# Batch 1's keys and values by plain transfers and halvings on GpSimd; batch 2's keys accumulated between the halvings

## The chip, the cores and the metric

The kernel runs on one core of a Trainium2 chip. The metric is the device time of one execution in microseconds (us); the time of a kernel is the median of its runs. The profile is of one execution, taken by the hardware profiler. Engines are called as the profile calls them: PE is TensorE's matmuls, PEld its weight loads, DVE is VectorE, ACT is ScalarE, POOL is GpSimd, SP is SyncE; the DMA queue that SP issues to is SPq.

## What is computed

Attention with pooled keys and values (8 batches, 8 heads, 576 tokens, 64 channels; groups of 8 keys and of 8 values are averaged, which leaves 72 of each), followed by a feed-forward layer with a squared ReLU, from 512 to 2048 and back to 512:

```python
Sp = S // pool                                    # 576 // 8 = 72
k_p = k.reshape(B, H, Sp, pool, D).mean(axis=3)
v_p = v.reshape(B, H, Sp, pool, D).mean(axis=3)
scores = scale * np.matmul(q, k_p.transpose(0, 1, 3, 2))
attn = np.exp(scores - np.max(scores, axis=-1, keepdims=True))
attn = attn / (np.sum(attn, axis=-1, keepdims=True) + 1e-09)
attn_out = np.matmul(attn, v_p).astype(np.float32)
x = np.ascontiguousarray(attn_out.transpose(0, 2, 1, 3)).reshape(B * S, H * D)
h = np.maximum(x @ w_in, 0.0)
out = (h * h @ w_out).astype(np.float32)
```

The two weight matrices come as 64-bit floats, so the kernel reads 16.8 MB of weights and makes float32 of them itself.

## The kernel before, in words

**Tiling.** The 4608 tokens are cut into 9 chunks of 512 (`c`). A chunk's feed-forward layer goes in 16 steps (`fc`), each for 128 of the 2048 hidden channels: `h_c_fc` is the product with `w_in`, `r` is ACT's ReLU and square of it, and `o` is the product with `w_out`, three steps later (`LAG`). A step `s` is `c * 16 + fc`. Step `s` issues on PE first `h` of step `s`, then the attention work that is due at `s`, then `o` of step `s - 3`. Chunk 0 lies wholly in batch 0; chunk 1 needs the last 64 tokens of batch 0 and 448 tokens of batch 1; chunk 2 needs batches 1 and 2.

**Weights.** The raw pieces, 512 KB each, are called `raw_i` (of `w_in`) and `raw_o` (of `w_out`), 32 in all. `land` loads one, `magnitude` has two ACT instructions on it, and `to_float32` three DVE instructions (one TENSOR_SCALAR and two SCALAR_TENSOR_TENSOR with two inputs each), which give `wf_i` or `wf_o`. Eight pieces are loaded ahead of all steps (`EAGER`); the others are due at steps that are worked out backwards from when PE needs them, two per step, loaded two or three steps ahead of their conversion.

**Order.** Every engine executes its instructions in the order in which they are written. In a step, the list `work` holds what is due; on DVE and ACT the attention's parts come first, then pooling, conversions and weights, and the ReLU of the step (`activate`) stands behind the step's `magnitude` calls. The SP queue too is in order: an issue that waits holds all behind it, and an issue waits until the transfer eight places ahead of it has landed (eight semaphores in turn).

**Keys and values.** Batch 0's come as whole rows (`load_pair`: tiles `k8`, `v8`, one for each pair of heads, 288 KB), and chunk 0's queries as four transfers `qn` of 256 KB between the first of them. DVE reduces three pairs of keys (`reduce_k`); POOL does the rest by halvings (`by_halves`: three additions a pair, over 512, 256 and 128 columns). From batch 1 on, the keys and values come as sums made by the DMA: `load_sums` loads one pair of rows of each group in a plain transfer (144 KB) and adds the other three with accumulating transfers, which POOL issues (`GP.dma_start`, tiles `k2`, `v2`, two halves `n` of four heads each), and `pool` adds the last two columns' halves on DVE. An accumulating transfer is issued only when the one before it on its half has landed. The pooled keys are `kq`, the pooled values `vp`. `turn_k` transposes the keys on PE (`kps`): at step 3 for batch 1, at step 8 for batch 2. Values of batch 1 are used on PE (`weigh_values`, `av`) from step 7 on, and the softmax weights `te` of chunk 1 are normalised on DVE at step 5 and transposed on PE (`pps`) at step 6. Scores of chunk 1 are `sps`.

**What is around the change.** The loads ahead of the steps stand in lines 686 to 702, the prologue's POOL work in lines 728 to 737, batch 1's accumulations of values and its two poolings in lines 789 to 794, and batch 2's and later batches' in `kv_steps` (lines 817 to 824). Most large tiles come from one pool of 40 buffers (`w_tile`, `SLOTS`), so that a later load can wait for the last reader of a buffer.

Of the kernel before, what the change touches and what calls it, by code (L numbers as in the profile page):

```python
# [9 lines left out]
F32 = mybir.dt.float32  # L10
# [27 lines left out]
def pooled_attn_relu2_ffn(  # L38
# [22 lines left out]
    POOL = 8  # L61
    SP_ = S // POOL
    NPAIR = H // 2
# [9 lines left out]
    PLAIN = 2  # L73
# [10 lines left out]
    EARLY = ((-13, -12, -8, -7), (0, 1, 2, 3, 4))  # L84
    HALF_AT = ((0, 1, 3, 6, 8), (1, 2, 5, 7, 9))
    KV_AT = (("k", -35), ("v", -27))
    NEXT_AT = {"k": ((3, 4, 5, 6, 7), (3, 4, 5, 6, 7)), "v": ((7, 8, 9, 11, 13), (7, 8, 10, 12, 14))}
    X_AT = (("B11", -9), ("B22", -2), ("T1", -2), ("T3", -2), ("T2", -1), ("B21", -1), ("T4", -1))
    STIR, AWAKE = 10, (2, 2, 0)

# [12 lines left out]
    def load(dst, src):  # L103
        loads.append((dst, src))
# [11 lines left out]
    def w_tile(dt, name):  # L116
        return wts.tile([P, 2, 512], dt, name=name, tag="w", bufs=SLOTS)
# [13 lines left out]
    def land(key):  # L131
        t = raw[key] = w_tile(U32, "raw_" + "_".join(map(str, key)))
        if key[0] == "i":
            _, g, kh, r = key
            n = GB * P
            load(t, w_in[kh * 2 * P:(kh + 1) * 2 * P, (2 * g + r) * n:(2 * g + r + 1) * n].rearrange("(c p) n -> p c n", p=P))
        else:
            load(t.rearrange("p a n -> p (a n)"), w_out[key[1] * P:(key[1] + 1) * P, :])
# [89 lines left out]
    def load_pair(kind, b, p):  # L228
        t = loaded[kind, b, p] = w_tile(F32, f"{kind}8_{b}_{p}")[:SP_]
        load(t, {"k": k, "v": v}[kind][b, 2 * p:2 * p + 2].rearrange("h (s o) d -> s h (o d)", o=POOL))  # L230
# [9 lines left out]
    def halve_k(b, p):  # L240
        if p == 0:
            loaded["kq", b] = sb.tile([SP_, H, D], F32, name=f"kq_{b}", tag="kq", bufs=1)
        kp = loaded["kp", b, p] = loaded["kq", b][:, 2 * p:2 * p + 2, :]
        by_halves(kp, loaded.pop(("k", b, p)))

    def halve_v(b, p):
        new_batch(b)
        by_halves(kv[b][:, 2 * p:2 * p + 2, :], loaded.pop(("v", b, p)))
# [7 lines left out]
    two, started, HALF = {}, set(), H // 2  # L256

    def load_sums(kind, b, n, j):

        if (kind, b) not in started:  # L260
            started.add((kind, b))
            if kind == "k":
                loaded["kq", b] = sb.tile([SP_, H, D], F32, name=f"kq_{b}", tag="kq", bufs=1)
        src = {"k": k, "v": v}[kind][b].rearrange("h (s j o) d -> j s h (o d)", j=POOL // 2, o=2)[j][:, n * HALF:(n + 1) * HALF]
        if b < PLAIN:
            if j == 0 and n == 0:
                t = w_tile(F32, f"{kind}2_{b}")
                for i in range(2):
                    two[kind, b, i] = t[:SP_, i, :].rearrange("s (h x) -> s h x", h=HALF)
            dst = two[kind, b, n]  # L270
        elif j == 0:
            dst = two[kind, b, n] = sb.tile([SP_, HALF, 2 * D], F32, name=f"{kind}2_{b}_{n}", tag="two", bufs=2)
        else:
            dst = two[kind, b, n]
        if j == 0:
            load(dst, src)
        else:
            GP.dma_start(dst, src, accum_op=ALU.add)
# [394 lines left out]
    steps = [(c, fc) for c in range(NCH) for fc in range(NFC)]  # L673
    work = {}

    def at(step, f, *a):
        work.setdefault(max(step, -PRO), []).append((f, a))
# [15 lines left out]
    load_pair("v", 0, 2)  # L693
    load_pair("v", 0, 3)
    land(keys[1])
    for n in range(2):
        load_sums("k", 1, n, 0)
    for key in keys[2:EAGER]:
        land(key)
    for n in range(2):  # L700
        load_sums("v", 1, n, 0)
    issue_loads()


# [23 lines left out]
    for p in range(3):  # L728
        reduce_k(0, p)
    halve_k(0, 3)  # L730
    more = [(n, j) for j in range(1, POOL // 2) for n in range(2)]
    for p in range(NPAIR):
        halve_v(0, p)
        if p == 1:
            load_sums("k", 1, *more.pop(0))
    for n, j in more:
        load_sums("k", 1, n, j)

    st = [None] * NPAIR
    st[0] = turn_rows(0, 0)  # L740
# [45 lines left out]
    to_float32(*keys[2:FIRST])  # L786
    begin(3)

    v_sums = [(n, j) for j in range(1, POOL // 2) for n in range(2)]
    for i, (n, j) in enumerate(v_sums):  # L790
        at(i // 2, load_sums, "v", 1, n, j)
    for n in range(2):
        at(2, pool, "k", 1, n)
        at(5, pool, "v", 1, n)
    at(3, turn_k, 1)
    at(6, split_k, 1)

# [1 line left out]
    t = 1e9  # L799
    for key in reversed(keys):  # L800
        t = min(t - 1 / RATE, need[key] - 1 - MARGIN)
# [15 lines left out]
    def kv_steps(b, s):  # L817
        for kind, start in KV_AT:
            for n in range(2):
                steps = NEXT_AT[kind][n] if b == PLAIN else [s + start + d for d in HALF_AT[n]]  # L820
                for j in range(POOL // 2):
                    at(steps[j], load_sums if j else first_sums, kind, b, n, j)
                at(steps[-1], pool, kind, b, n)
        at(8 if b == PLAIN else s + KV_AT[1][1] + 3, turn_k, b)
# [4 lines left out]
    for c in range(1, NCH):  # L829
# [10 lines left out]
        for p in range(NPAIR):  # L840
            s = c * NFC + first[p]
# [8 lines left out]
    for s in range(-PRO, len(steps) + LAG):  # L850
# [8 lines left out]
        if store:  # L859
            store()  # L860
            send_outs()
        store = project(*steps[s - LAG]) if s >= LAG else None
        if s % 2:
            catch_up()
        if soon:
# [66 lines left out]
```

## Time and profile before

| | us |
|---|---|
| median of 3 runs | 965.21 |
| lowest, highest | 958.71, 965.79 |
| time of the profiled execution | 962.24 |
| its span, first to last instruction | 960.5 |
| PE busy | 904.6 (94%) |
| DVE busy | 559.5 (58%) |
| ACT busy | 511.9 (53%) |
| POOL busy | 405.1 (42%) |

The mean granted TensorE clock of the profiled execution is 0.974 of full speed. Each timeline row has start, length, engine, line, operation, output and input tiles, shapes and count, and in brackets the idle time of the engine before it with what ended it. As nearly every instruction is issued through one helper, all have line 34: the tile names tell them apart. A row of the stretches has, for each engine, busy time and number of instructions, then the granted clock, the DMA engines' busy share and the rate in GB/s.

### The profile page before, as it was taken

The numbers are of one execution on the slowest core, as the hardware profiler recorded it, in microseconds if no ns is written. First come the engines' busy times: TensorE is split into PE (matmuls) and PEld (weight loads), VectorE is DVE, ScalarE is ACT, GpSimd is POOL, SyncE is SP. The second block draws the span as 40 slices with busy tenths as digits, with TensorE's granted clock in tenths as the row PEclk, the third lists the DMA queues.
The fourth block names the chain that finished last, engine by engine and source line by source line (L and its number), as shares of the span: only waits on it lengthen the run. The fifth ranks groups of instructions, "written<-read, shape, count | busy, mean of one in ns | idle before, by whom it ended". The sixth has DMA issues, their size and how long they took to land.

```text
span 960.5 us, 14101 instructions
## 1 busy us (share of the span) xinstructions
PE 904.6 (94%) x5082; PEld 719.8 (75%) x5082; DVE 559.5 (58%) x944; ACT 511.9 (53%) x1019; POOL 405.1 (42%) x215
## 2 busy tenths in 40 slices
PE   8809779999999899999999999999999999999998
PEld 5304334457777788888888888888888888889996
DVE  7705547745677787856575568556744563343321
ACT  5805436746555656565465546554654564444343
POOL 3412232545555446565665565656444444200000
PEclk8958889999999999999999999999999999999999
DMA  9986336468764655576657665755353443234501
GB/s 227 261 210 135 37 55 179 137 151 227 216 161 110 155 137 142 125 178 161 134 123 192 152 142 136 179 142 129 112 169 96 133 121 133 100 136 174 228 1 45
DMA packets 162088, 138.73 MB, mean 144 GB/s; under 512 B 95785, under 2 KB 128041, under 8 KB 162017
## 3 DMA queue, kind: packets, MB, share of 16 engines
q1 hardware_dynamic: 128416, 125.36, 43.4%
q0 software_dynamic: 33600, 12.46, 11.3%
q8 instruction: 40, 0.66, 0.3%
q14 instruction: 32, 0.25, 0.1%
HBM read 119.65 MB, written 18.06 MB: 143 GB/s over the span
## 4 chain that ended last, share of the span: by engine, by line
PE 69%; issue 9%; DVE 9%; DMA 6%; ACT 3%; POOL 3%; SPq 1%; DVEq 0%; ACTq 0%; POOLq 0%
PE o L34 34%; PE h L34 30%; DMA k<-in_k_dram 3%; PE sps L34 3%; PE av L34 2%; DMA w_o<-kept 2%; DVE wf_i L34 1%; POOL k L34 1%; POOL v L34 1%; DVE gl L34 1%; DVE xf L34 1%; DVE wf_o L34 1%; DVE st L34 1%; DMA rb<-rd 1%; ACT sc L34 1%
## 5 line engine op out<-in xcount | busy, mean ns | idle before, releaser
L34 PE MATMUL o<-w_o,gh 128*128 128x512 f32 x1024 | 322.2, 396 | 1.8 <-DMA w_o<-kept 1.7
L34 POOL PARTITION_ALL_REDUCE tot<-sc x56 | 190.1, 3443 | 85.0 <-issue 82.4
L34 PEld LDWEIGHTS o<-w_o,gh 128*128 128x128 f32 x1024 | 184.3, 188 | 46.8 <-issue 6.1
L34 PE MATMUL o<-w_o,gl 128*128 128x512 f32 x512 | 200.9, 392 | 0.0
L34 PE MATMUL h<-x_T,w_S 128*128 128x256 f32 x1008 | 130.9, 283 | 3.8 <-ACT r L34 3.0
L34 ACT ACTIVATE r<-h 128x512 f32<-128x512 f32 x144 | 83.4, 593 | 94.7 <-PE h L34 75.9
L34 POOL PARTITION_ALL_REDUCE mx<-sc x56 | 109.2, 1994 | 54.5 <-ACT sc L34 52.7
L34 PEld LDWEIGHTS h<-x_T,w_S 128*128 128x128 f32 x1008 | 125.0, 190 | 4.6 <-ACT r L34 3.2
L34 PEld LDWEIGHTS o<-w_o,gl 128*128 128x128 f32 x512 | 96.2, 188 | 21.1 <-DVE gl L34 0.2
L34 POOL DMA_DIRECT2D k<-in_k_dram x42 | 51.4, 1223 | 141.4 <-issue 91.7
L34 POOL DMA_DIRECT2D v<-in_v_dram x42 | 51.7, 1230 | 133.3 <-issue 57.0
L34 DVE TENSOR_TENSOR h<-h,u 128x256 f32<-128x256 f32 x168 | 72.7, 433 | 60.0 <-ACT u L34 31.7
L34 ACT COPY u<-h 128x256 f32<-128x256 f32 x112 | 41.8, 373 | 118.4 <-PE h L34 71.9
L34 PE MATMUL h<-x_B,w_A 128*128 128x256 f32 x672 | 98.6, 283 | 0.2 <-ACT r L34 0.2
L34 DVE TENSOR_TENSOR gl<-r,gh 128x512 fp32r<-128x512 f32 x128 | 94.4, 773 | 6.0 <-ACT gh L34 5.9
L34 PEld LDWEIGHTS h<-x_B,w_A 128*128 128x128 f32 x672 | 91.7, 189 | 5.3 <-ACT r L34 0.6
L34 ACT ACTIVATE r<-r 128x512 f32<-128x512 f32 x144 | 84.3, 625 | 1.1
L34 DVE TENSOR_TENSOR u<-h,u 128x256 f32<-128x256 f32 x56 | 23.4, 417 | 103.5 <-ACT u L34 103.5
L34 DVE TENSOR_TENSOR st<-qs,st 64x512 fp32r<-64x512 f32 x56 | 46.3, 826 | 58.7 <-ACT st L34 57.9
L34 ACT CAST gh<-r 128x512 fp32r<-128x512 f32 x128 | 78.9, 617 | 0.9 <-PE o L34 0.7
L34 ACT ACTIVATE sc<-sc 72x512 f32<-72x512 f32 x56 | 34.5, 632 | 67.2 <-DVE sc L34 67.2
L34 PE MATMUL o<-wf_o,r 128*128 128x512 f32 x128 | 64.3, 650 | 0.0
(93 smaller groups left out, 1183.4 us busy)
## 6 DMA issues: line engine op xcount, KB each, us to landing
w_o<-kept SPq DMA_DIRECT2D x128, 512.0 KB
out_dram<-ob SPq DMA_DIRECT2D x36, 256.0 KB
raw_i<-in_moe_w_in_dram SPq DMA_DIRECT2D x16, 512.0 KB
raw_o<-in_moe_w_out_dram SPq DMA_DIRECT2D x16, 512.0 KB
kept<-w_o SPq DMA_DIRECT2D x16, 512.0 KB
rb<-rd SPq DMA_DIRECT2D x56, 128.0 KB
k<-in_k_dram POOLq DMA_DIRECT2D x42, 144.0 KB, 5.4
v<-in_v_dram POOLq DMA_DIRECT2D x42, 144.0 KB, 5.5
```

Source lines behind the costliest of these rows:

```text
L34: return lambda *a, **k: self.tc.keep_in_program_order(f(*a, **k))
```

## The change

Batch 1's keys and values are loaded as whole rows, like batch 0's, behind the first eight weight pieces; POOL halves all eight pairs in the prologue. Batch 2's two plain key transfers move to the prologue as well, and their six accumulating transfers stand between and behind the halvings of batch 1's values. Of batch 2's keys only `pool` stays in the steps, at step 7 for both halves. In steps 0 and 1 the ReLU comes ahead of the step's `magnitude` calls.

```diff
-    NEXT_AT = {"k": ((3, 4, 5, 6, 7), (3, 4, 5, 6, 7)), "v": ((7, 8, 9, 11, 13), (7, 8, 10, 12, 14))}
+    NEXT_AT = ((7, 8, 9, 11, 13), (7, 8, 10, 12, 14))
...
-        if b < PLAIN:
-            if j == 0 and n == 0:
-                t = w_tile(F32, f"{kind}2_{b}")
-                for i in range(2):
-                    two[kind, b, i] = t[:SP_, i, :].rearrange("s (h x) -> s h x", h=HALF)
-            dst = two[kind, b, n]
-        elif j == 0:
+        if j == 0:
             dst = two[kind, b, n] = sb.tile([SP_, HALF, 2 * D], F32, name=f"{kind}2_{b}_{n}", tag="two", bufs=2)
...
     land(keys[1])
-    for n in range(2):
-        load_sums("k", 1, n, 0)
     for key in keys[2:EAGER]:
         land(key)
+    for p in range(NPAIR):
+        load_pair("k", 1, p)
+    for p in range(NPAIR):
+        load_pair("v", 1, p)
     for n in range(2):
-        load_sums("v", 1, n, 0)
+        load_sums("k", PLAIN, n, 0)
     issue_loads()
...
     halve_k(0, 3)
+    for p in range(NPAIR):
+        halve_v(0, p)
+    for p in range(NPAIR):
+        halve_k(1, p)
     more = [(n, j) for j in range(1, POOL // 2) for n in range(2)]
     for p in range(NPAIR):
-        halve_v(0, p)
-        if p == 1:
-            load_sums("k", 1, *more.pop(0))
+        load_sums("k", PLAIN, *more.pop(0))
+        halve_v(1, p)
     for n, j in more:
-        load_sums("k", 1, n, j)
+        load_sums("k", PLAIN, n, j)
...
-    v_sums = [(n, j) for j in range(1, POOL // 2) for n in range(2)]
-    for i, (n, j) in enumerate(v_sums):
-        at(i // 2, load_sums, "v", 1, n, j)
-    for n in range(2):
-        at(2, pool, "k", 1, n)
-        at(5, pool, "v", 1, n)
...
-                steps = NEXT_AT[kind][n] if b == PLAIN else [s + start + d for d in HALF_AT[n]]
+                if b == PLAIN and kind == "k":
+                    at(NEXT_AT[n][0], pool, kind, b, n)
+                    continue
+                steps = NEXT_AT[n] if b == PLAIN else [s + start + d for d in HALF_AT[n]]
...
         store = project(*steps[s - LAG]) if s >= LAG else None
+        if activate and s < 2:
+            activate()
+            activate = None
```

In the orders below, the numbers behind a name are batch and pair or half, and last the buffer's own number.

SP's queue before, from the second raw piece to the first that is due in the steps (`k2_1` and `v2_1` are the plain first transfers of batch 1's sums):

```order
L34 DMA raw_i_0_1_0_88<-in_moe_w_in_dram 128x2x512
L34 DMA k2_1_90<-in_k_dram 72x4x128 x2
L34 DMA raw_i_0_0_1_91<-in_moe_w_in_dram 128x2x512
L34 DMA raw_i_0_1_1_92<-in_moe_w_in_dram 128x2x512
L34 DMA raw_o_0_93<-in_moe_w_out_dram 128x1024
L34 DMA raw_o_1_94<-in_moe_w_out_dram 128x1024
L34 DMA raw_i_1_0_0_95<-in_moe_w_in_dram 128x2x512
L34 DMA raw_i_1_1_0_96<-in_moe_w_in_dram 128x2x512
L34 DMA v2_1_97<-in_v_dram 72x4x128 x2
L34 DMA raw_o_2_443<-in_moe_w_out_dram 128x1024
```

And now, from the eighth raw piece on:

```order
L34 DMA raw_i_1_1_0_94<-in_moe_w_in_dram 128x2x512
L34 DMA k8_1_0_95<-in_k_dram 72x2x512
L34 DMA k8_1_1_96<-in_k_dram 72x2x512
L34 DMA k8_1_2_97<-in_k_dram 72x2x512
L34 DMA k8_1_3_98<-in_k_dram 72x2x512
L34 DMA v8_1_0_99<-in_v_dram 72x2x512
L34 DMA v8_1_1_100<-in_v_dram 72x2x512
L34 DMA v8_1_2_101<-in_v_dram 72x2x512
L34 DMA v8_1_3_102<-in_v_dram 72x2x512
L34 DMA k2_2_0_104<-in_k_dram 72x4x128
L34 DMA k2_2_1_105<-in_k_dram 72x4x128
L34 DMA raw_o_2_483<-in_moe_w_out_dram 128x1024
```

Eight transfers of 288 KB and two of 144 KB now stand between the eighth raw piece and the ninth (`raw_o_2`), where two of 144 KB stood; the two that stood behind the second raw piece are gone.

POOL's order before, behind the second pair of batch 0's values:

```order
L34 DMA k2_1_90<-in_k_dram 72x4x128
L34 TENSOR_TENSOR v8_0_2_86<-v8_0_2_86 72x2x256
L34 TENSOR_TENSOR v8_0_2_86<-v8_0_2_86 72x2x128
L34 TENSOR_TENSOR vp_0_158<-v8_0_2_86 72x128
L34 TENSOR_TENSOR v8_0_3_87<-v8_0_3_87 72x2x256
L34 TENSOR_TENSOR v8_0_3_87<-v8_0_3_87 72x2x128
L34 TENSOR_TENSOR vp_0_158<-v8_0_3_87 72x128
L34 DMA k2_1_90<-in_k_dram 72x4x128 x5
L34 DMA v2_1_97<-in_v_dram 72x4x128 x6
L34 DMA k2_2_0_568<-in_k_dram 72x4x128
```

And now, from the last pair of batch 1's keys on:

```order
L34 TENSOR_TENSOR k8_1_3_98<-k8_1_3_98 72x2x256
L34 TENSOR_TENSOR k8_1_3_98<-k8_1_3_98 72x2x128
L34 TENSOR_TENSOR kq_1_185<-k8_1_3_98 72x128
L34 DMA k2_2_0_104<-in_k_dram 72x4x128
L34 TENSOR_TENSOR v8_1_0_99<-v8_1_0_99 72x2x256
L34 TENSOR_TENSOR v8_1_0_99<-v8_1_0_99 72x2x128
L34 TENSOR_TENSOR vp_1_199<-v8_1_0_99 72x128
L34 DMA k2_2_1_105<-in_k_dram 72x4x128
L34 TENSOR_TENSOR v8_1_1_100<-v8_1_1_100 72x2x256
L34 TENSOR_TENSOR v8_1_1_100<-v8_1_1_100 72x2x128
L34 TENSOR_TENSOR vp_1_199<-v8_1_1_100 72x128
L34 DMA k2_2_0_104<-in_k_dram 72x4x128
```

Twelve accumulating transfers of batch 1 are gone from POOL's queue, 24 additions have come in, and batch 2's six follow the keys of batch 1 instead of its values.

ACT's order before, where the first ReLU stands:

```order
L34 ACTIVATE wf_o_0_440<-raw_o_1_94 128x512
L34 ACTIVATE raw_o_1_94<-raw_o_1_94 128x512
L34 ACTIVATE wf_i_1_0_449<-raw_i_1_0_0_95 128x2x256
L34 ACTIVATE raw_i_1_0_0_95<-raw_i_1_0_0_95 128x512
L34 ACTIVATE r_0_0_459<-h_0_0_385 128x512
L34 ACTIVATE r_0_0_459<-r_0_0_459 128x512
```

And now:

```order
L34 ACTIVATE r_0_0_485<-h_0_0_425 128x512
L34 ACTIVATE r_0_0_485<-r_0_0_485 128x512
L34 ACTIVATE wf_o_0_480<-raw_o_1_92 128x512
L34 ACTIVATE raw_o_1_92<-raw_o_1_92 128x512
L34 ACTIVATE wf_i_1_0_490<-raw_i_1_0_0_93 128x2x256
L34 ACTIVATE raw_i_1_0_0_93<-raw_i_1_0_0_93 128x512
```

The first ReLU has moved ahead of four ACT instructions, and the second likewise; PE's order is the same as before, and DVE's lacks four additions, batch 1's poolings.

## The prediction

> **What bounds the kernel now.** I read PE's waits first (waiting instruction, what it waited for, us in all, times, longest; from 40 us on), then stretches of the span, then the rows around each wait.
>
> ```profile
> PE kps L34 <- DVE kq L34: 29.8, 4, 20.8
> PE pps L34 <- DVE te L34: 6.3, 1, 6.3
> PE h L34 <- ACT r L34: 4.2, 3, 3.0
> PE o L34 <- DMA w_o<-kept: 1.7, 4, 0.8
> ```
>
> ```profile
> 0.00:30.00 30.00, 24.41 (x143) 14.55 (x144) 24.26 (x44) 17.99 (x55) 14.09 (x18) 0.89 0.93 251
> 30.00:45.00 15.00, 14.00 (x43) 5.62 (x42) 11.46 (x21) 12.32 (x23) 4.17 (x5) 1.00 0.92 231
> 45.00:65.00 20.00, 2.57 (x6) 0.78 (x5) 0.00 (x0) 2.80 (x6) 2.39 (x2) 0.65 1.05 272
> 65.00:130.00 65.00, 46.32 (x154) 21.80 (x154) 27.73 (x57) 25.37 (x56) 16.46 (x14) 0.84 0.44 76
> 140.00:300.00 160.00, 156.69 (x653) 102.53 (x652) 107.27 (x163) 97.06 (x186) 76.52 (x39) 1.00 0.63 168
> 300.00:950.00 650.00, 644.52 (x4043) 565.88 (x4042) 380.14 (x644) 348.47 (x682) 288.24 (x136) 1.00 0.51 137
> ```
>
> From 140 us PE is busy nearly all the time at full clock, so what PE gains before then is kept at the end. Between 45 and 65 us PE, DVE and ACT stand nearly still. The rows name the cause:
>
> ```profile
> 61.26 1.19 POOL L34 DMA_DIRECT2D k<-in_k_dram  x1 [11.23 <-issue]
> 67.83 0.42 DVE L34 TENSOR_TENSOR kq<-k 72x256 f32<-72x256 f32 x1 [25.62 <-DMA k<-in_k_dram]
> 68.40 0.47 PE L34 MATMUL kps<-ident,kq 72*128 72x72 f32 x2 [20.83 <-DVE kq L34]
> 72.54 0.50 PE L34 MATMUL kps<-ident,kq 72*128 72x72 f32 x2 [3.67 <-DVE kq L34]
> 98.69 0.42 DVE L34 TENSOR_TENSOR vp<-v 72x256 f32<-72x256 f32 x1 [5.97 <-DMA v<-in_v_dram]
> 105.26 1.89 PE L34 MATMUL pps<-ident,te 128*72 128x128 f32 x8 [6.33 <-DVE te L34]
> 124.40 0.32 PE L34 MATMUL kps<-ident,kq 72*128 72x72 f32 x2 [0.47 <-DVE kq L34]
> 129.52 0.50 PE L34 MATMUL kps<-ident,kq 72*128 72x72 f32 x2 [4.80 <-DVE kq L34]
> ```
>
> The three accumulating transfers per half run one after the other while the weights fill the DMA engines (share 1.05). POOL idles 11.23 us between two of them, DVE is held at the pooling of batch 1's keys, and PE at their transposes. The same chain, delayed, holds DVE at batch 1's values (so `te` is late for `pps`, step 6) and PE at batch 2's keys (step 8).
>
> **What goes.** Batch 1's twelve accumulating transfers and its four poolings on DVE: the waits 20.83 + 3.67, and 6.33, since DVE then meets nothing it waits for at step 5. Batch 2's six accumulating transfers follow batch 1's keys, so they are done some 50 us earlier, and 0.47 + 4.80 goes. Together 36.1 us. After each such wait PE runs at half clock for a while:
>
> ```profile
> 72.84 6.32 PE L34 MATMUL o<-wf_o,r 128*128 128x512 f32 x8
> 106.95 4.58 PE L34 MATMUL o<-wf_o,r 128*128 128x512 f32 x8
> 114.80 1.04 PE L34 MATMUL pps<-ident,te 128*72 128x128 f32 x8
> 115.77 1.09 PE L34 MATMUL av<-sc,vp 72*64 72x64 f32 x8
> 129.95 1.98 PE L34 MATMUL av<-sc,vp 72*64 72x64 f32 x8
> 131.85 5.86 PE L34 MATMUL o<-wf_o,r 128*128 128x512 f32 x8
> 142.19 3.70 PE L34 MATMUL o<-wf_o,r 128*128 128x512 f32 x8
> ```
>
> Against the 3.70 of an undisturbed `o` the three cost 2.62 + 0.88 + 2.16; `av` costs 0.89 more than at 115.77, `pps` (1.89) 0.85 more than at 114.80, and the two `kps` of 0.50, against 0.32, some 0.4. That is 7.8 us.
>
> ```profile
> 39.77 0.61 ACT L34 ACTIVATE r<-h 128x512 f32<-128x512 f32 x1
> 40.44 7.13 PE L34 MATMUL h<-x,wf_i 128*128 128x512 f32 x16 [1.00 <-ACT r L34]
> 45.48 0.66 ACT L34 ACTIVATE wf_i<-raw_i 128x512 f32<-128x512 f32 x1
> ```
>
> The earlier ReLU removes the 1.00 us that `h` of step 2 waits for `r`; the four ACT instructions it passes move behind it, and their weights are wanted only from step 4 on. So the gross gain is 36.1 + 7.8 + 1.0 = 44.9 us, and the profiled execution's 962.24 would become 917.3.
>
> **What comes in: POOL.** Durations of the halvings in the first 40 us, one row for each of the three additions (mean ns), and last the shortest of each, from the keys:
>
> ```profile
> L34 POOL TENSOR_TENSOR v<-v 72x512 f32<-72x512 f32 x4 | 5.5, 1383 | 0.3 <-DMA v<-in_v_dram 0.3
> L34 POOL TENSOR_TENSOR v<-v 72x256 f32<-72x256 f32 x4 | 3.6, 908 | 0.3
> L34 POOL TENSOR_TENSOR vp<-v 72x128 f32<-72x128 f32 x4 | 2.9, 736 | 0.3
> L34 POOL TENSOR_TENSOR k<-k 72x512 f32<-72x512 f32 x1 | 1.3, 1267 | 12.3 <-DMA k<-in_k_dram 12.3
> L34 POOL TENSOR_TENSOR k<-k 72x256 f32<-72x256 f32 x1 | 0.7, 726 | 0.1
> L34 POOL TENSOR_TENSOR kq<-k 72x128 f32<-72x128 f32 x1 | 0.5, 455 | 0.1
> 31.00 0.85 POOL L34 TENSOR_TENSOR vp<-v 72x128 f32<-72x128 f32 x1
> ```
>
> A pair takes 3.03 us on average, 2.45 at least. Batch 0's values end at 31.85. Ahead of batch 1's keys SP issues 7.60 MB (batch 0's eight loads of 0.295, its four of queries of 0.262, eight weight pieces of 0.524), with them 8.78. By the rates of the stretches 7.53 MB have landed at 30 us, so the last keys land near 30 + 1.25 / 0.231 = 35.4. POOL then ends them at 31.9 + 4 x 3.03 = 44, where PE wants them when `h` of step 3 ends, near 47. I book 1 us of wait for a slower POOL. Four values pairs and the first four accumulating transfers at 1.2 us each end near 44 + 12.1 + 4.8 = 61 if none waits; they are wanted at step 7, some 80 us, as steps without waits take about 8 us (`h` and `o` at 3.5 from the start of one to that of the next, and attention). Behind POOL's additions the SP queue waits too: pieces due at steps 6 and 7 take over buffers of batch 1's keys and values. At 61 us that costs nothing; the cover is a step and a half.
>
> **The weights behind 2.1 MB more.** The piece that ACT converts at 45.48 (`raw_i` for step 6) has 9.76 MB up to and with it now, 11.83 then; at 45 us 11.0 MB have landed, so it lands at 45.8 (with 272 GB/s from 30 us on) to 48.1. ACT's next ReLU, at 46.6 now, goes up to 2.6 us later; PE needs it for `h` of step 4, near 51. Cost 0, and with that cover gone 2.6.
>
> **DVE beside POOL.** This is the unknown. DVE's conversions meet POOL's additions only at one place of the trace:
>
> ```profile
> 24.29 3.14 DVE L34 SCALAR_TENSOR_TENSOR wf_i<-wf_i,raw_i 128x512 uint32<-128x512 uint32 x1
> 27.46 1.10 DVE L34 SCALAR_TENSOR_TENSOR wf_i<-raw_i,wf_i 128x512 uint32<-128x512 uint32 x1
> 22.36 0.76 DVE L34 TENSOR_TENSOR te<-te,tm 128x576 f32<-128x576 f32 x1
> L34 DVE TENSOR_TENSOR te<-te,tm 128x576 f32<-128x576 f32 x4 | 4.6, 1145 | 0.1
> L34 DVE SCALAR_TENSOR_TENSOR wf_i<-wf_i,raw_i 128x512 uint32<-128x512 uint32 x4 | 2.7, 687 | 0.1
> ```
>
> The last row is of 32 to 47 us, where POOL adds nothing: 0.69. Beside additions the two rows average 2.12, 1.43 more; the four `te`, three of them beside additions, 0.39 more than 0.76. POOL's work from 32 us on covers some five steps with 20 such conversions, so DVE gets 8 to 29 us more to do. From 140 to 300 us DVE is busy 107.27 of 160 us, so I give it a slack of a third, 2.6 us of a step of 8, 13 in all. PE is thus held 0 to 16 us; I take 4, nearer to the row with four cases, mainly at `h` of steps 2 and 4, whose weights are converted just ahead. With POOL's 1 us that makes 5.
>
> The Trainium skill, "SBUF — State Buffer", section "Who interferes with whom", says that a DVE instruction with two SBUF inputs contends with a GpSimd instruction that reads SBUF, and that this is an exclusive lock: one waits for the other to finish. The 3.14 agrees in kind but is longer than one addition. By that rule each conversion would wait at most one addition, 1.01 us on average, 20 us in all, 7 beyond the slack, and the time would be 924.
>
> **The sum.** 962.24 - 44.9 + 5 = 922.3 against the profiled execution. That one lies 3.0 below the median of the runs (965.21), so the median comes out between 922 and 925; I say 924. Its own range goes from 917, no new wait, to 933, DVE's 16.
>
> **Rivals.**
>
> *The weights come late (0.14).* If the ninth to eleventh piece have no reserve at 45 us, the whole 2.07 MB at 272 GB/s count: PE is held 7.6 us more, and at half clock for an `o` behind it (2.6): 934. For it: DMA is full over the first 65 us. Against it: the 9.76 MB above, landed some 6 us early.
>
> *POOL is late (0.14).* With the longest pair, 3.7 us, and keys at 40 us, they end at 55: 8 us of wait and 2.6 of clock. The values and batch 2's sums follow, and a wait like today's 4.80 at step 8 stays: 940. For it: the accumulating transfers wait 11.23 us when DMA is full, and now stand ahead of batch 1's values.
>
> *The wait goes over to SP (0.05).* If those transfers hold POOL twice by 11.23 us, the last values pair is done at 83 instead of 61, the weight piece of step 8 is issued only then, and the queries behind it: some 13 us at step 7 and as much again at steps 8 and 9 with the clock: 947 to 955.
>
> *DVE starves and the kernel gets slower (0.05).* If every conversion beside POOL takes 3.14, and POOL's 24 additions are held by 0.69 each, the overlap lasts seven steps: 28 x 2.45 = 69 us, less 18 of slack, 51 on PE: 968, and more with the clock. It decides once conversions average above 2.9 us. Against it stand the 1.10 and the `te` row.
>
> **How the numbers follow.** The forecast has 0.62. The range goes from 914, below the gross gain by the scatter between runs, to 942, which takes in the first two rivals, and leaves out the last two and the tails of the others, under 0.2. About 1% is what a measurement of this kernel can tell from no change (958.71 to 965.79 before). Faster by over 1% hold the forecast, the first two rivals and the lower part of the third, 0.91; within 1% its upper part and mild forms of the fourth, 0.05; slower the rest, 0.04.
>
> **What would show it.** Right: no `kps` wait above 3 us and no `pps` wait; clock near 1.00 from 65 to 140 us; batch 1's `kq` on POOL ended by 48 us; the first row of a PE wait after 40 us naming DVE's `wf_i`. Wrong: POOL idle behind batch 2's accumulating transfers with SP waiting for it, ACT's `magnitude` waiting for `raw` pieces, conversions above 1.7 us on average from 32 to 65 us, or PE waits beyond 140 us that before did not show.

## The result and the profile after

The changed kernel takes 923.33 us (median of 4 runs, 920.41 to 924.9), the kernel before, on the same chip, 965.2. The ratio is 0.958, with a 95% interval of 0.954 to 0.962. In a later comparison the changed kernel took 924.54 (5 runs, 920.4 to 925.54) against 963.2, a ratio of 0.959 (0.956 to 0.962). Forecast were 924, within 914 to 942. The profiled execution takes 923.48, its span is 921.7; the granted clock over the span went from 0.974 to 0.989.

PE's waits, over the whole span (instruction, what it waited for, us in all, times, longest):

```profile
PE h L34 <- ACT r L34: 4.5, 3, 3.0
...
PE h L34 <- DVE wf_i L34: 2.7, 1, 2.7
```

The `kps` waits of 29.8 us and the `pps` wait of 6.3 are gone, all of them. The 3.0 for `r` stood there before as well. New are 1.32 for `r` and 2.70 for `wf_i`, shown below.

Stretches of the span, columns as before:

```profile
0.00:30.00 30.00, 24.31 (x138) 15.13 (x140) 21.33 (x42) 14.93 (x49) 13.99 (x19) 0.77 0.93 245
30.00:45.00 15.00, 15.00 (x46) 6.15 (x45) 13.06 (x17) 13.00 (x25) 10.09 (x10) 1.00 0.91 226
45.00:65.00 20.00, 15.98 (x58) 7.07 (x57) 20.00 (x20) 9.53 (x17) 15.29 (x15) 1.00 1.00 249
65.00:92.00 27.00, 27.00 (x99) 12.84 (x98) 22.79 (x44) 21.47 (x49) 6.90 (x7) 1.00 0.81 213
...
100.00:260.00 160.00, 156.78 (x656) 102.74 (x655) 111.42 (x165) 97.37 (x186) 77.88 (x40) 1.00 0.65 169
```

From 45 to 65 us PE is busy 15.98 us where it was 2.57, at a granted clock of 1.00 instead of 0.65, and DVE, which stood still there, is now busy all 20 us. The last row is the stretch from 140 us of before, 40 us earlier: nothing in it has changed (156.78 of 160 us against 156.69).

PE's timeline of the changed kernel at the places where the waits were:

```profile
47.65 0.42 PE L34 MATMUL kps<-ident,kq 72*128 72x72 f32 x4
47.91 3.65 PE L34 MATMUL o<-wf_o,r 128*128 128x512 f32 x8
52.87 1.98 PE L34 MATMUL h<-x,wf_i 128*128 128x512 f32 x4 [1.32 <-ACT r L34]
57.55 1.98 PE L34 MATMUL h<-x,wf_i 128*128 128x512 f32 x4 [2.70 <-DVE wf_i L34]
75.72 1.04 PE L34 MATMUL pps<-ident,te 128*72 128x128 f32 x8
92.42 0.42 PE L34 MATMUL kps<-ident,kq 72*128 72x72 f32 x4
93.79 3.70 PE L34 MATMUL o<-wf_o,r 128*128 128x512 f32 x8
```

Each `kps`, `pps` and `o` that stood behind a wait now has its undisturbed length (3.65 and 3.70 for `o`, against 6.32 and 5.86). PE reaches batch 1's keys at 47.65, practically when it did before (68.40 less the wait of 20.83 is 47.57), and batch 2's at 92.42 instead of 124.40. So the change in span splits into three stretches:

| us | before | after | gain | booked |
|---|---|---|---|---|
| start to batch 1's first `kps` | 47.57 | 47.65 | -0.1 | 1.0 |
| from there to batch 2's first `kps` | 76.83 | 44.77 | 32.1 | 31.3 of waits + 4.5 of clock - 5 = 30.8 |
| from there to the end of the span | 836.1 | 829.3 | 6.8 | 4.8 of waits + 3.3 of clock = 8.1 |
| span | 960.5 | 921.7 | 38.8 | 39.9 |

The first row needs two more rows of PE's timeline, the last `pps` of batch 0, of the kernel before:

```profile
32.04 1.04 PE L34 MATMUL pps<-ident,te 128*72 128x128 f32 x8
```

and of the changed kernel:

```profile
33.45 1.04 PE L34 MATMUL pps<-ident,te 128*72 128x128 f32 x8
```

The changed kernel's execution came there 1.4 us later (its clock in the first 30 us was 0.77, that of before 0.89) and gained 1.3 us between there and the keys. The start differs from execution to execution without any edit in it: in the kernel with the late ReLU, below, these 30 us had a granted clock of 0.96. The last stretch, too, has a scatter: in seven executions of the changed kernel and of variants of it, it took 826.0 to 829.4 us. Most of that is the clock: PE waits 3.00 us for `r` there in all seven (up to 274.74 us in the changed kernel), and behind it the granted clock was halved for 6.83 us in the executions with 829.3 and 829.4, for 3.41 us in those with 827.4 and 828.5, and not at all in those with 826.0, 827.0 and 827.5. The kernel before waits as long there and kept its clock. A profile's total is thus good to some 3 us.

What POOL does now:

```profile
34.44 2.08 POOL L34 TENSOR_TENSOR k<-k 72x512 f32<-72x512 f32 x2 [5.77 <-DMA k<-in_k_dram]
...
46.84 0.52 POOL L34 TENSOR_TENSOR kq<-k 72x128 f32<-72x128 f32 x1
...
48.43 2.85 POOL L34 TENSOR_TENSOR v<-v 72x512 f32<-72x512 f32 x2
...
69.39 1.21 POOL L34 DMA_DIRECT2D k<-in_k_dram  x1 [6.23 <-issue]
...
72.80 0.85 POOL L34 TENSOR_TENSOR vp<-v 72x128 f32<-72x128 f32 x1
```

POOL waits 5.77 us for the first pair of keys and ends the fourth at 47.36, 0.3 us before PE's first `kps` at 47.65. The accumulating transfers of batch 2 hold it 6.23 us at one place, so batch 1's values end at 73.65; PE weighs them from about 84 us on. The last accumulating transfer is issued at 79.35, in time for DVE's pooling at 86.8.

And ACT, whose rows explain the wait for `r`:

```profile
47.58 0.69 ACT L34 ACTIVATE wf_o<-raw_o 128x512 f32<-128x512 f32 x1 [1.77 <-DMA raw_o<-in_moe_w_out_dram]
51.12 0.67 ACT L34 ACTIVATE wf_i<-raw_i 128x512 f32<-128x512 f32 x1 [0.43 <-DMA raw_i<-in_moe_w_in_dram]
52.25 0.57 ACT L34 ACTIVATE r<-h 128x512 f32<-128x512 f32 x1
```

The ninth weight piece comes at 47.6, the eleventh at 51.1, and the ReLU that `h` of step 4 waits for stands behind it: 52.25, where it was 46.6 before.

### The profile page after: what moved, and what is told of

Read it like the earlier page. It is cut to its first block, busy times and chain, and to the rows that moved or that the text cites. A ratio compares the mean times of both kernels' runs of the same rounds, so it can differ in the third digit from the quotient of the medians.

```text
span 921.7 us, 14113 instructions
## 1 busy us (share of the span) xinstructions
PE 900.1 (98%) x5080; PEld 720.1 (78%) x5082; DVE 570.9 (62%) x940; ACT 512.4 (56%) x1019; POOL 416.3 (45%) x227
## 4 chain that ended last, share of the span: by engine, by line
PE 78%; DVE 10%; DMA 4%; ACT 3%; issue 2%; SPq 1%; DVEq 0%; ACTq 0%
PE o L34 37%; PE h L34 34%; PE sps L34 4%; PE av L34 3%; DVE wf_i L34 2%; DMA w_o<-kept 2%; DVE gl L34 1%; DVE wf_o L34 1%; SPq L34 1%; DVE xf L34 1%; PE pps L34 1%; DMA qn<-in_q_dram 1%; ACT sc L34 1%; DVE vp L34 1%; DMA kept<-w_o 1%
## 5 line engine op out<-in xcount | busy, mean ns | idle before, releaser
L34 POOL DMA_DIRECT2D v<-in_v_dram x36 | 44.0, 1222 | 114.4 <-issue 50.4
L34 DVE TENSOR_TENSOR gl<-r,gh 128x512 fp32r<-128x512 f32 x128 | 91.5, 750 | 5.7 <-ACT gh L34 5.6
L34 POOL DMA_DIRECT2D k<-in_k_dram x36 | 44.3, 1230 | 97.8 <-issue 46.8
L34 PE MATMUL h<-x,wf_i 128*128 128x512 f32 x128 | 58.2, 597 | 5.3 <-DVE wf_i L34 2.7
```

The lines of the kernel that those rows point to most:

```text
L34: return lambda *a, **k: self.tc.keep_in_program_order(f(*a, **k))
```

## Experiments

Two questions were to be settled. First, whether the waits and the clock behind them are the whole gain, and which part of the change brings which share: I took the waits for one chain of accumulating transfers that moves on to the next user unless all of it goes. Rivals were that one part alone brings it all, and that the clock behind a wait has no price of its own. Second, what the remaining 4 us are: DVE slowed by POOL's additions, weights that come late, or POOL's keys.

### Batch 1's keys alone

The kernel before with batch 1's keys in plain transfers and halved on POOL; values and batch 2 as before.

```diff
     land(keys[1])
-    for n in range(2):
-        load_sums("k", 1, n, 0)
     for key in keys[2:EAGER]:
         land(key)
+    for p in range(NPAIR):
+        load_pair("k", 1, p)
...
-        if p == 1:
-            load_sums("k", 1, *more.pop(0))
-    for n, j in more:
-        load_sums("k", 1, n, j)
+    for p in range(NPAIR):
+        halve_k(1, p)
...
-        at(2, pool, "k", 1, n)
```

> The kernel before with the keys' part of the change alone: batch 1's keys come as four plain loads behind the first eight weight pieces and are halved on GpSimd; batch 1's values and batch 2's keys are accumulated by DMA as before. Theory (a chain of accumulating transfers moves on when one chain is removed): the waits of 20.8 and 3.7 us at step 3 go, but the values' chain starts on POOL near 47 us in a DMA that is full, so DVE waits some 8 to 15 us at step 5 and PE's wait at pps grows from 6.3 to about 10; batch 2's keys still hold PE 3 to 5 us. 935 to 945. Rival (each wait is its own and only the keys' one is removed): 24.5 us of wait and 2.9 of clock go, the others stay as they are: 933 to 936 with pps at 6.3 and kps of batch 2 at 4.8.

Measured: 948.38 us, ratio 0.985 (0.977 to 0.993). The keys' `kps` waits for nothing. PE's timeline at the next wait and, below it, DVE's:

```profile
90.32 1.89 PE L34 MATMUL pps<-ident,te 128*72 128x128 f32 x8 [18.22 <-DVE te L34]
```

```profile
83.61 0.42 DVE L34 TENSOR_TENSOR vp<-v 72x256 f32<-72x256 f32 x1 [17.73 <-DMA v<-in_v_dram]
```

Of 24.50 us of waits at the keys, 11.89 came back at the values (18.22 instead of 6.33), since DVE was now held 17.73 us at their pooling. The chain moves on, further than I had expected: keys alone are worth some 15 us (7 to 22 by the interval), about a third of the change.

### Batch 2's keys accumulated in the steps again

The changed kernel, with batch 2's keys loaded and accumulated at steps 3 to 7 as before the change.

```diff
-    NEXT_AT = ((7, 8, 9, 11, 13), (7, 8, 10, 12, 14))
+    NEXT_AT = {"k": ((3, 4, 5, 6, 7), (3, 4, 5, 6, 7)), "v": ((7, 8, 9, 11, 13), (7, 8, 10, 12, 14))}
...
-    for n in range(2):
-        load_sums("k", PLAIN, n, 0)
...
     for p in range(NPAIR):
-        load_sums("k", PLAIN, *more.pop(0))
         halve_v(1, p)
-    for n, j in more:
-        load_sums("k", PLAIN, n, j)
```

> The changed kernel with batch 2's keys where they were before: plain transfers at step 3, accumulating ones at steps 4 to 7 behind all of batch 1's halvings, pooling at step 7. Theory A (the prediction's term: batch 2's earlier start is worth the wait of 5.3 us and 2.5 of clock): kps of batch 2 waits 4 to 6 us, clock falls behind it, 928 to 932. Theory B (batch 2 was late only because batch 1's transfers stood ahead of it on POOL): POOL is free at about 62 us, six transfers at 4.2 us end near 88, DVE's pooling at 86 to 87 waits 0 to 2 us, PE's kps not at all; the time is that of the changed kernel, 920 to 925.

Measured: 931.7 us, ratio 0.968 (0.964 to 0.972), 8.4 above the changed kernel. POOL's timeline, then PE's:

```profile
66.00 1.52 POOL L34 DMA_DIRECT2D k<-in_k_dram  x1 [4.46 <-DMA k<-in_k_dram]
...
93.71 1.20 POOL L34 DMA_DIRECT2D k<-in_k_dram  x1 [2.82 <-issue]
```

```profile
93.99 0.47 PE L34 MATMUL kps<-ident,kq 72*128 72x72 f32 x2 [4.50 <-DVE kq L34]
98.55 0.50 PE L34 MATMUL kps<-ident,kq 72*128 72x72 f32 x2 [4.09 <-DVE kq L34]
```

POOL has no additions left after 61 us, and still the issues of the six transfers stretch from 66 to 94 us. PE waits 8.6 us for them and runs at half clock behind them (the next `o` takes 5.26), some 11 us in all by the rows; the medians differ by 8.4. So the earlier place of these six is worth 8 us or more by itself. Booked for them were 0.47 + 4.80 of waits and about 3 of clock; they are that late even with batch 1's transfers out of the way.

### POOL halves the values before the keys

```diff
+    for p in range(NPAIR):
+        halve_v(1, p)
     for p in range(NPAIR):
         halve_k(1, p)
...
         load_sums("k", PLAIN, *more.pop(0))
-        halve_v(1, p)
```

> The changed kernel with POOL halving batch 1's values ahead of its keys, batch 2's accumulating transfers behind both. In the changed kernel the keys are done at 47.36 us and PE wants them at 47.65, a margin of 0.3. Theory (POOL is as near to the bound as that): the keys are done four pairs later, at about 60 to 63; PE waits 13 to 15 us at batch 1's kps and runs at half clock for the o behind it (2.6), less the 4.0 us that it waits at step 4 now: 933 to 938. Rival (PE would have to wait there anyway, for weights and conversions at step 4, so that most of a late kps is hidden): under 6 us more, 924 to 929.

Measured: 939.09 us, ratio 0.975 (0.971 to 0.980), 15.8 above the changed kernel. PE's waits:

```profile
PE kps L34 <- POOL kq L34: 19.0, 4, 10.9
```

The waits of step 4 are gone in this run: a PE that comes 19 us later finds weights and conversions done. The net of the two, with an `o` of 6.47 instead of 3.65 behind the last wait, is 19.0 - 4.0 + 2.8 = 17.8, within this comparison's interval of the 15.8. POOL's margin at the keys is thus small, and their place ahead of everything else on POOL matters; part of the lateness is that POOL stood idle for 13.79 us, until the values had landed.

### The clock alone

The kernel before, with identity products in PE's four long waits, whose results nothing uses, so that the waits stay and the clock behind them does not fall. First with 170, 28, 50 and 38 products:

```diff
+    WARM = {(1, 0): 170, (1, 2): 28, (2, 2): 38}
+    WARM_P = 50
...
+            for _ in range(WARM.get((b, j), 0)):
+                PE.matmul(pt[:, 384:], lhsT=ident, rhs=ident, start=True, stop=True)
...
+        for _ in range(WARM_P if (c, p) == (1, 0) else 0):
+            PE.matmul(pt[0][:, 384:], lhsT=ident, rhs=ident, start=True, stop=True)
```

> The kernel before, with 286 matmuls of the identity tile (128x128, results unused) put on PE just ahead of the four places where it waits: 170 ahead of batch 1's first key transposes, 28 ahead of their second half, 38 ahead of batch 2's second half, 50 ahead of the transposes of chunk 1's softmax weights. At about 0.105 us each they fill most of each wait and lengthen none. Theory of the prediction (the waits also cost 7.8 us of half clock behind them): the waits' ends stay where they are, the clock stays near 1.00 from 70 to 140 us, each o behind a wait takes 3.70, and the time falls by about 7.8, to some 955 to 957. Rival (the long o rows have another cause, the same transfers or a busy DVE): the o rows keep 6.3, 4.6 and 5.9 us and the time stays within 2 us of before.

Measured: 985.72 us, ratio 1.024 (1.019 to 1.029). The first of the four rows of the products:

```profile
49.87 38.13 PE L34 MATMUL kps<-ident 128*128 128x128 f32 x340
```

Each product ran as two passes of 0.112 us, twice what I had meant, so the four blocks (38.13, 6.46, 11.33 and 8.70, 64.6 us) overran the waits they stood in (35.6) by 29.0. The time rose by 22.6 only. The difference, 6.4 us, is what the clock would explain, for which 7.8 was booked, but the interval of this ratio is 5 us to either side. As the blocks had a length of their own here, I repeated it with half as many (`WARM` 88, 15, 20 and `WARM_P` 27):

> The kernel before, with identity products (results not used) in PE's four long waits, half as many as in the run with too many of them: 88 ahead of batch 1's first kps, 15 ahead of its third, 27 ahead of pps, 20 ahead of batch 2's third kps, which at the 0.112 us of a pass and two passes each last 19.7, 3.4, 6.0 and 4.5 us, a little less than the waits of 20.83, 3.67, 6.33 and 4.80. The waits stay, as work; only the clock behind them changes. Theory: the half clock behind the waits costs 7.8 us. The rows of o behind them take 3.6 to 3.7 us instead of 6.32, 4.58 and 5.86, and the time is 955 to 958 against 963 of the kernel before. Rival: the next wait takes the gain back, since batch 1's values and batch 2's keys arrive by transfers, not by PE's time: the rows of o are short, the waits for te and kq are longer by as much, and the time is 961 to 964.

Measured: 963.04 us, ratio 1.000 (0.997 to 1.002): no difference. PE's timeline:

```profile
78.43 3.64 PE L34 MATMUL o<-wf_o,r 128*128 128x512 f32 x8
...
101.69 6.19 PE L34 MATMUL pps<-ident 128*128 128x128 f32 x54
110.72 1.07 PE L34 MATMUL pps<-ident,te 128*72 128x128 f32 x8 [2.84 <-DVE te L34]
111.62 5.29 PE L34 MATMUL o<-wf_o,r 128*128 128x512 f32 x8
...
135.88 3.70 PE L34 MATMUL o<-wf_o,r 128*128 128x512 f32 x8
```

Here the rival is right. The first `o` took 3.64 instead of 6.32, and the wait for `te` took 9.03 (6.19 of products, 2.84 idle) instead of 6.33: the 2.7 us gained were waited for at the next place, which hangs on transfers and not on PE (from batch 1's last `kps` to this `pps` it is 32.4 us, before 32.7). Behind the 2.84 us that stayed idle the clock fell again, and the second `o` took 5.29, not less than the 4.58 of before, so this run says nothing of the clock there. Only the third `o` (3.70 instead of 5.86) has no such wait behind it to give its gain to; 2 us are within this comparison's interval. So the clock term could be added in the sum only because the next wait went too. By these rows, a change that removed the first wait alone would have got nothing for its clock.

### One addition a pair

The additions over 512 and 256 columns of batch 1's halvings are left out.

```diff
-    def by_halves(dst, src):
+    def by_halves(dst, src, n=POOL * D // 2):
...
-        n = POOL * D // 2
...
-        by_halves(kp, loaded.pop(("k", b, p)))
+        by_halves(kp, loaded.pop(("k", b, p)), D if b else POOL * D // 2)
```

> The changed kernel, in which each halving of batch 1's keys and values is cut to its last addition, over 128 columns; the additions over 512 and 256 columns are left out for batch 1, so six of each group's eight rows are not added. All transfers and everything else stay. It takes away most of POOL's additions while DVE converts. Theory: DVE's additional wait is made by POOL's additions. The two-input conversions between 32 and 65 us average below 0.8 us (1.14 in the changed kernel, 0.69 before the change), the wait of h for wf_i (2.7 us) is gone, the wait for r at step 4 (1.3 us, ACT behind late weights) stays; kps never waits; the time is 919 to 922. Rival: the conversions are longer for another reason, the full DMA writing into the same memory: they stay near 1.1 us, and the time stays at 923 to 925.

Measured: 922.73 us, ratio 0.957 (0.954 to 0.961), the changed kernel's time. DVE's conversions with two inputs between 32 and 65 us in the changed kernel (count, busy time, mean ns):

```profile
L34 DVE SCALAR_TENSOR_TENSOR wf_i<-wf_i,raw_i 128x512 uint32<-128x512 uint32 x6 | 7.8, 1312 | 0.2 <-ACT raw_i L34 0.2
L34 DVE SCALAR_TENSOR_TENSOR wf_o<-wf_o,raw_o 128x512 uint32<-128x512 uint32 x4 | 5.7, 1416 | 0.1
L34 DVE SCALAR_TENSOR_TENSOR wf_i<-raw_i,wf_i 128x512 uint32<-128x512 uint32 x6 | 5.6, 945 | 0.0
L34 DVE SCALAR_TENSOR_TENSOR wf_o<-raw_o,wf_o 128x512 uint32<-128x512 uint32 x4 | 3.7, 915 | 0.0
```

and without the two longer additions, with PE's wait in the same kernel below:

```profile
L34 DVE SCALAR_TENSOR_TENSOR wf_i<-wf_i,raw_i 128x512 uint32<-128x512 uint32 x7 | 4.7, 683 | 0.1
L34 DVE SCALAR_TENSOR_TENSOR wf_i<-raw_i,wf_i 128x512 uint32<-128x512 uint32 x6 | 4.3, 727 | 0.0
```

```profile
54.59 6.70 PE L34 MATMUL h<-x,wf_i 128*128 128x512 f32 x8 [3.54 <-ACT r L34]
```

The cause of DVE's slowness is settled: without the additions a conversion takes 0.68 to 0.73 again instead of 1.14 on average, under a DMA that is nearly as full (shares of 0.89 and 0.92 from 30 to 45 and 45 to 65 us, against 0.91 and 1.00), and no `h` waits for `wf_i`. What that is worth in the time is not shown: the 2.7 us in question are less than the intervals of both medians. By the rows, `h` of step 4 now waits 3.54 for `r`, which stands behind weights that landed 1.4 us later than in the changed kernel's profile (48.94 instead of 47.58), and runs at half clock behind it. The late weights and the slowed DVE lie beside each other at step 4; by these rows, taking one away leaves the other.

### Weights ahead of batch 1's values, conversions one piece after the other, both

The first kernel lands three more weight pieces ahead of batch 1's values:

```diff
+    for key in keys[EAGER:EAGER + 3]:
+        land(key)
     for p in range(NPAIR):
         load_pair("v", 1, p)
...
-        if i >= EAGER:
+        if i >= EAGER + 3:
```

> The changed kernel with the ninth to eleventh weight piece loaded between batch 1's keys and its values. In the changed kernel ACT waits 3.8 us in all for these pieces (47.58 to 51.12 us) and for the next, and PE waits 1.32 us for r at step 4. Theory (weights behind the values are late): ACT's waits for these three pieces go, PE's 1.32 goes, 2.70 stays or grows by up to 1: the time falls by about 1. Rival (values later mean POOL later and the gain is lost at the buffers SP waits for): POOL ends 3 to 5 us later, time unchanged or up to 3 us more.

The second has DVE finish one piece before the next:

```diff
-        for _, m, _ in parts:
+        for words, m, bits in parts:
             DVE.tensor_scalar(m, m, EXP_MIN, EXP_MAX, op0=ALU.max, op1=ALU.min)
-        for words, _, m in parts:
-            DVE.scalar_tensor_tensor(m, m, 3, words[..., 0], op0=ALU.logical_shift_left, op1=ALU.bitwise_or)
-        for words, _, m in parts:
-            DVE.scalar_tensor_tensor(m, words[..., 1], 0x80000000, m, op0=ALU.bitwise_and, op1=ALU.bitwise_or)
+            DVE.scalar_tensor_tensor(bits, bits, 3, words[..., 0], op0=ALU.logical_shift_left, op1=ALU.bitwise_or)
+            DVE.scalar_tensor_tensor(bits, words[..., 1], 0x80000000, bits, op0=ALU.bitwise_and, op1=ALU.bitwise_or)
```

> The changed kernel with to_float32 converting one piece after the other instead of taking turns between two. PE's longest new wait (2.70 us at h of step 4) is for a wf_i whose last conversion stands behind the first conversion of a wf_o that took 2.47 us beside POOL's additions. Theory (DVE beside POOL holds PE there): that wf_i is ready 2.5 to 3 us sooner, the 2.70 goes, the time falls by 2 to 3. Rival (the wait is the weights' lateness, through ACT): the wait moves to r and the time stays.

The third has both edits:

> Both of the two edits before together (conversions one by one, three weight pieces ahead of batch 1's values). If both theories hold, no wait above 1 us is left on PE in steps 2 to 8 and the time falls by 3.5 to 4, to about 919; if PE's wait at step 4 only changes its name, it stays.

and beside them ran the changed kernel:

> The changed kernel itself, on the chip of the next three, so that they can be compared with it: 920 to 925.

| | us (median) | ratio (95%) |
|---|---|---|
| changed kernel | 924.54 | 0.959 (0.956 to 0.962) |
| weights ahead of values | 920.85 | 0.956 (0.952 to 0.959) |
| one piece after the other | 921.49 | 0.958 (0.954 to 0.962) |
| both | 919.93 | 0.955 (0.951 to 0.958) |

The changed kernel's second profile, from this comparison, has the same two waits in other sizes, 2.26 instead of 1.32 and 1.03 instead of 2.70:

```profile
53.30 1.98 PE L34 MATMUL h<-x,wf_i 128*128 128x512 f32 x4 [2.26 <-ACT r L34]
56.31 1.98 PE L34 MATMUL h<-x,wf_i 128*128 128x512 f32 x4 [1.03 <-DVE wf_i L34]
```

Rows of PE's timeline, the longest waits between 40 and 65 us, with the weights ahead, then with one piece after the other, then with both:

```profile
54.19 1.98 PE L34 MATMUL h<-x,wf_i 128*128 128x512 f32 x4 [1.70 <-DVE wf_i L34]
```

```profile
52.78 3.70 PE L34 MATMUL h<-x,wf_i 128*128 128x512 f32 x8 [1.18 <-ACT r L34]
57.82 1.18 PE L34 MATMUL sps<-kf,st 64*64 64x72 f32 x20 [1.34 <-DVE st L34]
```

```profile
49.51 0.28 PE L34 MATMUL kps<-ident,kq 72*128 72x72 f32 x1 [2.28 <-POOL kq L34]
49.63 5.34 PE L34 MATMUL o<-wf_o,r 128*128 128x512 f32 x8
```

With the weights earlier the wait for `r` is gone, and the one for `wf_i` is left. With the conversions in another order the wait for `wf_i` is gone, and `r` is left, with a new one for DVE's `st` and 0.96 us for POOL's keys. With both, neither is left, but POOL's keys hold PE 2.28 us, and the `o` behind takes 5.34 instead of 3.65: 4.0 us in all, as much as the two waits of the changed kernel. The medians of the three lie 3 to 5 us below the changed kernel's, but the intervals of all four overlap, so none is shown to be faster. The waits can be told apart, since each names its cause: steps 3 and 4 hold some 2 to 4 us under three causes, of which another is last in each kernel. As the two profiles of one kernel differ by 0.9 and 1.7 us at these places, a single wait's size here is not settled by one execution.

### The ReLU back in its place

```diff
-        if activate and s < 2:
+        if activate and s < 0:
```

> The changed kernel, with the ReLU of steps 0 and 1 back behind the step's magnitude calls. Theory: the early ReLU is worth the 1.0 us booked for it. h of step 2 waits about 1.0 us for r again, as before the change (1.00), everything else stays, and the time is 924 to 926, against 923 to 924.5. Rival: h of step 2 is followed by the wait at step 4 (1.3 us for r, 2.7 for wf_i), so a PE that comes there 1 us later waits 1 us less, and nothing is lost: 922 to 924 with the wait at step 2 back and those behind it smaller by as much.

Measured: 924.54 us, ratio 0.960 (0.957 to 0.963). ACT's timeline, then PE's:

```profile
48.34 0.67 ACT L34 ACTIVATE wf_o<-raw_o 128x512 f32<-128x512 f32 x1 [6.64 <-DMA raw_o<-in_moe_w_out_dram]
```

```profile
39.93 3.70 PE L34 MATMUL h<-x,wf_i 128*128 128x512 f32 x8 [0.97 <-ACT r L34]
50.09 6.06 PE L34 MATMUL h<-x,wf_i 128*128 128x512 f32 x8 [6.46 <-ACT r L34]
```

The wait of 0.97 is back, as expected. Not expected by either theory is the 6.46 behind it: the next ReLU now stands behind the ninth weight piece, which ACT waits 6.64 us for. Against the changed kernel this place costs 0.97 + 6.46 + 2.36 of clock, less the 4.0 us of waits at step 4, which are not there any more: 5.8. From batch 0's last `pps` to batch 2's first `kps` this kernel takes 64.6 us and the changed one 59.0. In the medians 0 to 1.2 us of that are seen, but their intervals are too wide to exclude 5.8. In the profile the rest stands elsewhere: the first 30 us ran at a clock of 0.96 instead of 0.77, so that batch 0's last `pps` came 1.9 us earlier, and the last stretch was 3.3 us shorter, without the 6.83 us of half clock that the changed kernel's profile had there. That the early ReLU protects PE from the late weights is shown by the rows; that it is worth 5.8 us in the time is not.

## Why the prediction was right

**What goes.** All three waits went, with the half clock behind them. In the stretch that holds batch 1, 32.1 us were gained and 4.0 of new waits paid, so 36.1 gross, where 31.3 + 4.5 were booked. The single parts show that the steps belong together: keys alone give 15 us, batch 2's earlier accumulation 8, the clock alone nothing that this comparison's 2.4 us to either side would show; batch 1's values with the early ReLU are the 16.7 us between 948.38 and 931.70, which no run takes alone.

**The clock term, 7.8.** Right for this change, for a reason that the prediction hadn't named. The run with products as long as the waits shows that PE's gain behind the first wait is given back at the next one, which hangs on transfers.

**The earlier ReLU, 1.0.** Right between 33 and 47 us (1.3), and mis-explained: I called it a wait of 1.0 removed, with weights "wanted only from step 4 on" behind it. Its larger effect is that the ReLU no longer stands behind a weight piece that lands at 48 us.

**POOL, booked 1.** Measured 0, with 0.3 us to spare, and that 0 is luck of one execution: in the profiles of four variants that leave batch 1's keys as they are, PE waited 0.29, 0.96, 2.28 and 2.29 us for them. The result hides that POOL came 3.4 us later than worked out. I let it start batch 1's keys at 31.9, when batch 0's values end; the first pair landed only at 34.4, and POOL waited 5.77 for it. Four pairs took 12.9 us, near the 12.1 of the mean price, so they ended at 47.4 and not at 44. The reserve of 3 us up to the 47 that PE wanted them at paid for it. A late POOL (the rival with 0.14) is what the run with the values first shows: 19 us of waits.

**Batch 1's values, 61 us.** They ended at 73.65. I had booked the accumulating transfers at 1.2 us each, "if none waits", and they did: 1.1, 1.1 and 6.2 us. That is the mechanism of the third rival at half its size, and the weight piece that waits for it on SP's queue was issued only at 73.67. It cost nothing: the values were wanted at about 84, and PE is busy all of the stretch from 65 to 92 us.

**Weights behind 2.1 MB more, booked 0.** Here a term was mis-sized. I expected the piece at 45.8 to 48.1; ACT got it at 51.1. The rate of 272 GB/s that I used (from 30 us on for the early end, from 45 for the late one) was not there: 245 in the first 30 us, 226 from 30 to 45 and 249 from 45 to 65, with which 11.83 MB are through at 49.4. That queries and accumulating transfers took the rest is likely, but not shown. It cost 1.32 us by the trace and 2.26 in the second profile, within the 2.6 that the text gave for the case that the cover is gone; in the run with one addition it cost 3.54 and the clock behind it.

**DVE beside POOL, booked 4.** Measured 2.70 (1.03 in the second profile), at `h` of step 4, as said; step 2 was not touched, since POOL began 2.5 us later. The 20 two-input conversions between 32 and 65 us average 1.14 us (1.31 in the second profile), 0.45 (0.62) above the 0.69, against the 1.43 and 0.39 between which I had chosen. The Trainium skill's rule ("SBUF — State Buffer", section "Who interferes with whom") would have given 7 through one whole addition for each conversion (924 for the profiled execution, where the sum had 922.3); on average they waited about half an addition of 1.01 us.

**The signs.** Of those named for right, one failed: the first wait of PE after 40 us names ACT's `r`, and `wf_i` only the second. Of those named for wrong, two came: POOL idle behind batch 2's transfers with SP waiting for it, and ACT's `magnitude` waiting for `raw` pieces (1.77, 0.59 and 0.43 us). They cost 0 and 1.32 us.

The sum of new waits was 4.0 against 5 booked (3.3 in the second profile), and of it 1.3 (2.3) stood under a cause booked at 0. The rest, 1.1 us between the 38.8 us of span gained and the 39.9 booked, is within the scatter of the first and the last stretch.

## What to carry to other kernels

A wait on a chain of serial transfers is not one wait: before removing it, follow the chain to its next users, and count the gain, and the clock behind it, only up to the first user that still hangs on it. Work that is off the critical path with room to spare may well go to another engine, as the halvings did, but the landing of its first operands and its place in that engine's queue then decide whether it is in time. When several causes end within 2 us of one another, removing one can leave the wait to another; here three such edits each left or brought another wait, and the medians could not tell their times apart.

## What the runs showed of the hardware

**The longest conversions on DVE begin beside POOL's issue of a transfer and end with the addition behind it.** DVE's timeline of the changed kernel, then POOL's, with the first of its two additions alone:

```profile
47.83 2.86 DVE L34 SCALAR_TENSOR_TENSOR wf_i<-wf_i,raw_i 128x512 uint32<-128x512 uint32 x1
```

```profile
47.31 1.51 POOL L34 DMA_DIRECT2D k<-in_k_dram  x1
48.43 1.71 POOL L34 TENSOR_TENSOR v<-v 72x512 f32<-72x512 f32 x1
```

The conversion ends at 50.7, 0.56 us behind the first addition (50.14) and inside the second. That is the time of one addition and not of two; it is longer than an addition because it began 0.6 us ahead of it, and why it did not end in these 0.6 us the rows don't say. All 14 two-input conversions of over 1.8 us up to 80 us, in seven profiles, the 3.14 of the kernel before among them, begin while POOL issues an accumulating transfer, and end 0.56 us behind the addition that follows. Where no issue stands ahead of an addition (the runs with batch 2's keys in the steps and with the values first), none of 32 to 65 us takes more than 1.77; beside an issue with no addition behind it they take at most 0.71. An instruction with a single input from SBUF was held too: a TENSOR_SCALAR took 2.51 us from 59.22 on instead of 0.49, and ended 0.29 behind the addition. The Trainium skill's rule of a lock between the two engines fits these rows ("SBUF — State Buffer", section "Who interferes with whom", which counts such an instruction among those that can take the shared port).

**Whether a gap of 2.3 us on PE halves its clock depends on where it falls.** The kernel with both edits ran an `o` of 5.34 behind a gap of 2.28, quoted above; the one with batch 2's keys in the steps, at the same place behind 2.29, one of 3.65. In all 13 profiles the granted clock changes only at points of a grid of 3.413 us, which begins elsewhere in each execution. Two stretches between such points in the kernel with both edits, columns as before, PE busy 1.13 of 3.41 us in the first, and the clock 0.50 in the second:

```profile
47.13:50.54 3.41, 1.13 (x6) 0.55 (x5) 3.29 (x4) 2.85 (x6) 2.17 (x3) 1.00 0.63 137
50.54:53.95 3.41, 3.41 (x6) 1.32 (x5) 1.92 (x4) 0.00 (x0) 2.09 (x2) 0.50 0.44 76
```

| kernel | PE's gap | idle within one stretch of the grid | clock in the next |
|---|---|---|---|
| batch 2's keys in the steps | 45.65 to 47.94 | 1.91 (46.03 to 49.45) | 1.00 |
| changed | 54.85 to 57.55 | 1.93 (55.62 to 59.04) | 1.00 |
| both edits | 47.23 to 49.51 | 2.28 (47.13 to 50.54) | 0.50 |
| half as many products | 107.88 to 110.72 | 2.34 (108.38 to 111.79) | 0.50 |

From 28 us on, each stretch at full clock with more than 1.94 us idle was followed by half clock, in all 13 profiles, and none with less than 1.91. The gap of 2.70, divided into 0.77 and 1.93 by the grid, thus cost its own length, and the one of 2.28 within a single stretch 4.0 us.

**Accumulating transfers are slow without a full DMA too.** With batch 1's twelve gone, batch 2's six, issued in the steps, took 4.0 to 7.5 us from one issue to the next. The stretch in that kernel:

```profile
65.00:95.00 30.00, 24.96 (x86) 11.82 (x86) 15.03 (x31) 18.97 (x40) 7.51 (x6) 0.98 0.74 173
```

The DMA engines were busy for a share of 0.74 there, against 1.05 where POOL waited 11.23 us before the change.
